# A fused attention and two expert layers on one core: decoding steps re-paced, two sums moved to VectorE, and the experts' ScalarE and VectorE put in program order

## The chip, the cores and the metric

One Trainium2 chip, one of its cores. The metric is the device time of the whole program in microseconds, from one launch. A chip core has five engines with a queue each: TensorE (PE; its weight loads are shown as PEld), VectorE (DVE), ScalarE (ACT), GpSimd (POOL) and SyncE (SP), which here only issues transfers.

## The reference, cut to what matters

Windowed attention with 32 global tokens per head feeds a dense two-matrix layer with a leaky activation, whose rows are routed to eight experts of equal capacity. Everything has fp32 inputs; `w_in`, `w_out` and `alpha` come as doubles.

```
x = attention(q_l, k_l, v_l, q_g, k_g, v_g)       # 2176 tokens x 512
h = x @ w_in                                      # 512 -> 2048
x = (max(h, 0) + alpha * min(h, 0)) @ w_out       # 2048 -> 512
logits = x @ w_gate                               # 8 experts
# pairs (token, expert) in falling order of their logit; a token takes the first
# expert that has room, and an expert has room for N / 8 = 272 tokens
for e in range(8):
    out[mask_e] = max(x[mask_e] @ w1[e], 0) @ w2[e]   # 512 -> 1024 -> 512
```

## The kernel before, in words

**Numbers.** A product of fp32 values is made from three products in the matmul's rounded type: high by high, high by low, low by high. The high half is a ScalarE copy into that type, the low half the difference of value and high half; `split` issues both, the difference on VectorE or, with `lo_eng=P`, on POOL. A weight or an activation that PE is to use is split once. The 2176 tokens are worked on in eight chunks of 272 (`CH`, also an expert's capacity, `CAP`).

**Stages.** Attention runs up to about 146 us, with the first half of the dense layer's weights decoded beside it. Then comes the dense layer's first half (hidden columns 0 to 1023): `gemm` makes, for each chunk, eight blocks of first products (12 matmuls each, L211), the activation (`neg` on ScalarE, `g` on VectorE, `ghi` on ScalarE, `glo` on POOL), and then the second products (L251): f 0 to 5 for each of four output blocks, and then f 6 and 7 for each, whose results leave as `xd` through two buffers to memory. The second half of the hidden columns follows in pairs of chunks by seven products instead of eight (`step`, L864), for which sums of quarters of the weights and of the activations are needed. Its second products (`gemm2b`, L1564; for the last chunk `last`, L1641) add to the stored part and write the rows out, turned by PE. Then each expert's slot (`slot`) makes 96 matmuls of first products (`up`, L1409) and 96 of second (`down`, L1429), eight slots in all.

**Decoding.** The doubles of the second half's weights are decoded in steps beside the dense first half: a ScalarE absolute value, then four VectorE operations on 128x512 integers, then for the quarters of `w_in` casts and differences. `parts` lists 24 such pieces; `work()` runs one step of the oldest. `turned_part` ends in two PE works of its own (L161, L168). The loop at L789 draws one point after another from `gemm`, each `yield` being one; from chunk 1 on each point adds to `due`, and if `due` is at least 1 it loses 1 and one step is issued. There are 16 points in a chunk's first products and 16 in its second, 172 steps in all.

**The first pair of chunks.** `start2` runs as the last chunk's second products begin. It lists, in `first2`, the operands and sums that the first pair of chunks of the seven products needs (`operand`: a split of 128x544 with the difference on POOL; `add2`: two sums of 128x544 on POOL), and the second products of the last chunk take one entry off at each point after f 1, 3 and 5.

**Order.** In attention PE, VectorE and ScalarE keep program order (`manual_schedule`), and from then on PE does to the end. In the dense first half and the seven products VectorE, ScalarE and POOL do too. After `order.close()` a planner orders VectorE, ScalarE and POOL by its own estimate of when an instruction can run. SP is always ordered by it. What an engine finds in its queue it runs in that order, and waits if the next is not ready.

**The router** is a generator (`router`, `phase`, `listing`) that is advanced beside the products: `advance(dt)` is called with the estimated time of what was issued, 0.113 for a matmul. An expert is closed after six rounds of two small PE works (`pc`, `pa`, L1238 and L1250) with VectorE work between them; at the end of the last round, `phase` issues a group of some twenty small VectorE operations and the next expert's best choice, then waits 2.7 for two more PE works (`pq`, L1297), and issues a second group that ends in a comparison of 128x1071 (`against`, L1204).

**Expert weights.** `fetch_1(k)` loads `w1` of an expert in four pieces of 128x1024 (512 KB each) into `raw3`, which has three buffers, and splits each (cast on ScalarE, difference on POOL); `fetch_2(k)` does so with `w2`. Both issue all four loads and splits at once: expert 0's from chunk 4 and chunk 6 of the second products on (counted from 0), expert 1's after `last`, the others as soon as the router has closed the expert and a buffer is free. `gather(k)` turns an expert's rows (L1389) through the one buffer `tx` of the pool `qx` and splits them (`xsh` on ScalarE, `xsl` on VectorE); `rows`, `tails` and `emit` (L309, L318, L1452) turn other rows through that same buffer. Four banks hold the results of `up` and `down`, in turn.

**Names of the change's steps:** `gemm1` L203, `gemm` L219, `add2` L276, `start2` L290, the pacing loop L789, `fetch_1` L1354, `fetch_2` L1368, `slot` L1488, the loop over the second products' chunks L1673, and the loop over the slots L1707.

Of the kernel before, what the change touches and what calls it, by code (L numbers as in the profile page):

```python
# [25 lines left out]
def tile_attention_moe_moe(ctx: ExitStack, tc: tile.TileContext, qkw, vw,  # L26
# [176 lines left out]
    def gemm1(c, f, g):  # L203
        _, xh, xl = X[c]
        pool, tag = odd[0] if odd and f % 2 else (pH, "h1")
        ps = pool.tile([128, CH], F32, name="h1", tag=tag)
        fs = slice(f * 128, (f + 1) * 128)
        i = 0
        for k in range(KD):
            for w, x in ((0, xh), (0, xl), (1, xh)):  # L210
                T.matmul(ps, WI[w][:, k, fs], x[:, k], start=i == 0, stop=i == 3 * KD - 1)  # L211
                i += 1
            if k % 2 == 1 and k < KD - 1:
                yield 0.7
        neg = gh_.tile([128, CH], F32, name="neg")
        A.activation(out=neg, in_=ps, func=AF.Relu, scale=-1.0)
        V.scalar_tensor_tensor(g, neg, al1[:, f:f + 1], ps, op0=OP.mult, op1=OP.add)

    def gemm(c, nxt):  # L219
# [8 lines left out]
        for f in range(KH):  # L228
            g = gh_.tile([128, CH], F32, name="g")
            yield from gemm1(c, f, g)  # L230
            split(gh[:, f], gl[:, f], g, lo_eng=P)
            yield 0.7
        if c + 1 in X:
# [9 lines left out]
        for d, fs in parts2:  # L243
            if d not in ys:
                pool, tag = (pY, "y") if d < 2 or not odd else (pH, "h1") if d == 2 else odd[0]
                ys[d] = pool.tile([128, CH], F32, name="y", tag=tag)
            ps = ys[d]
            ds_ = slice(d * 128, (d + 1) * 128)
            for f in fs:
                for i, (w, x) in enumerate(((0, gh), (0, gl), (1, gh))):  # L250
                    T.matmul(ps, WO[w][:, f, ds_], x[:, f], start=f == 0 and i == 0, stop=f == KH - 1 and i == 2)  # L251
                if f % 2 == 1 and f < KH - 1:
                    if first2 and nxt is None:
                        first2.pop(0)()
                    yield 0.7
            if fs[-1] < KH - 1:
                continue
            xd = gx.tile([128, CH], F32, name="xd", bufs=2)
            A.copy(xd, ps)  # L259
            nc.sync.dma_start(out=xpart[d, :, c * CH:(c + 1) * CH], in_=xd)  # L260
            yield 0.7
        X[c] = None
# [12 lines left out]

    def add2(i):  # L276
        a11, a12, a21, a22 = (quarter(k, t) for t in range(2) for k in range(2))
        if not i:
            P.tensor_tensor(sums[0], a21, a22, op=OP.add)
            P.tensor_tensor(sums[1], sums[0], a11, op=OP.subtract)  # L280
        else:
            P.tensor_tensor(sums[2], a11, a21, op=OP.subtract)
            P.tensor_tensor(sums[3], a12, sums[1], op=OP.subtract)

# [5 lines left out]
    def start2():  # L290
        tmp2.append(wa.tile([128, 15, CH], F32, name="tmp", tag="wa0b"))
        sums.extend(tmp2[0][:, 2 * i:2 * i + 2] for i in range(4))
        slots_.extend(gx.tile([128, 2, 2, CH], F32R, name="op", tag=t) for t in ("xh", "xl"))
        x = gx.tile([128, 2, 2, 2, CH], F32R, name="op", tag="xb1")
        slots_.extend(x[:, i] for i in range(2))
        first2.extend([lambda: operand(0, 0), lambda: operand(0, 1), lambda: add2(0), lambda: operand(0, 2),
                       lambda: operand(0, 3), lambda: add2(2)])

# [462 lines left out]
    with tc.tile_pool(name="dc2", bufs=1, side="right") as dc, tc.tile_pool(name="pW", bufs=2, space=PSUM) as pW, \  # L761
# [27 lines left out]
        while c < NCH:  # L789
            if g is None:  # L790
                g = gemm(c, c + 1 if c + 1 < NCH else None)
            while next(g, None) is not None:
                if c:
                    due += 0.82
                if due >= 1.0:
                    due -= 1.0
                    work()
            g = None
            c += 1
# [3 lines left out]
    with ExitStack() as mo:  # L803
# [542 lines left out]
        def fetch_x(k):  # L1346
# [5 lines left out]
            SLOT[k]["xg"] = xg  # L1352

        def fetch_1(k):  # L1354
            er = nc.values_load(EID[0:1, k:k + 1], engines=[mybir.EngineType.SP], min_val=0, max_val=E - 1)
# [6 lines left out]
            for kk in range(KD):  # L1362
                raw = rw.tile([128, FF], F32, name="raw3")
                nc.sync.dma_start(out=raw, in_=w1e[:, kk])
                split(t1[0][:, kk], t1[1][:, kk], raw, lo_eng=P)
            SLOT[k] = dict(w1=t1, er=er)

        def fetch_2(k):  # L1368
# [7 lines left out]
            for kk in range(0, K3, 2):  # L1376
                raw = rw.tile([128, 2, DM], F32, name="raw3")
                nc.sync.dma_start(out=raw, in_=w2e[:, kk:kk + 2])
                split(hi[:, kk:kk + 2], lo[kk // 2], raw, lo_eng=P)
            SLOT[k]["w2"] = [[hi[:, f] for f in range(K3)], [lo[f // 2][:, f % 2] for f in range(K3)]]  # L1380
# [107 lines left out]
        def slot(k):  # L1488
# [3 lines left out]
            if k == E - 1:  # L1492
                d["o"] = sl.tile([128, K3 + DM // 32, 32], F32, name="otl", tag="ot")
            f = 0
            if k == 0:
                yield from up(k, (0, 1), range(KD - 1), (0, 2))
# [3 lines left out]
            for f in range(f, K3):  # L1500
                yield from up(k, (f,), range(KD))
                if f % 2 == 0:
                    yield next(em, 0)
            d["up"] = True
            if k == E - 2:
                SLOT[k + 1]["w2f"] = wa.tile([128, K3, DM], F32, name="m2f", tag="wa1")
                w2e = w2[bass.ds(SLOT[k + 1]["er"], 1)].rearrange("e (k p) f -> p (e k) f", p=128)
                nc.sync.dma_start(out=SLOT[k + 1]["w2f"], in_=w2e)
# [78 lines left out]
        def last():  # L1587
# [71 lines left out]
            yield 0.0  # L1659

        sx = mo.enter_context(tc.tile_pool(name="sx", bufs=1))
        with tc.tile_pool(name="gb_", bufs=1) as gb_:
# [10 lines left out]
            for j, c in enumerate(ORD):  # L1673
                if j == NCH - 1:
                    while listed[0] < 1:
                        force()
                if j < NCH - 2:
                    reload(ORD[j + 2])
                for x in gemm2b(c) if j < NCH - 1 else last():
                    if j or not post:  # L1680
                        advance(x)
                    if closed[0] >= 1 and j >= 4 and 0 not in SLOT:
                        fetch_1(0)
# [3 lines left out]
        sl = mo.enter_context(tc.tile_pool(name="sl", bufs=1))  # L1687
        with tc.issue_after(SLOT[0]["cast"].ins):
            while closed[0] < 2:
                force()  # L1690
            fetch_1(1)

# [14 lines left out]
        for k in range(E):  # L1707
# [3 lines left out]
            for x in slot(k):  # L1711
                advance(x)
                n += x
                ahead(k, n)
# [4 lines left out]
                if gath is not None:  # L1719
                    left -= x  # L1720
                    if left <= 0:
                        y = next(gath, 0)
                        left = 2.2
                        n += y
                        advance(y)
            if k + 1 < E:
                while listed[0] < k + 2:
                    force()
                ahead(k, n)
                for x in gath or gather(k + 1):  # L1730
                    advance(x)


# [78 lines left out]
```

## Time and profile before

| | us |
|---|---|
| median of 3 runs (lowest, highest) | 806.62 (806.51, 807.21) |
| the profiled execution, by its own time | 805.96 |
| its span, first to last instruction | 803.9 |
| PE busy | 760.8 |
| VectorE busy | 483.5 |
| ScalarE busy | 403.5 |
| POOL busy | 413.7 |

The busy times are unions over the span. A stretch less PE's busy time in it is what PE stood idle; matmuls follow each other before the one in front has drained, so the end of each is a model, and a wait looks a little shorter than it is. The granted clock of TensorE is shown as a share of 2.4 GHz; it was 0.99 over the span. In a timeline the bracket behind a row gives how long the engine was idle before it and what ended that.

### The profile page before, as it was taken

To read this page: it belongs to the slowest core of one execution; us is meant where nothing else is said; L and a number is where in the kernel's file an instruction comes from. 1 tells how busy PE (TensorE), PEld (TensorE's weight loads), DVE (VectorE), ACT (ScalarE), POOL (GpSimd) and SP (SyncE) were. 2 spreads that over 40 slices of the span, in tenths; PEclk is the share of its full clock that TensorE was granted. 3 is DMA by queue.
4 is the path that set the end of the run, shared out by engine and by line. 5 is a ranking of instruction groups with operands and counts; after the bars stand their busy time and mean duration, and the time that the engine had idled before them with its cause. 6 is when DMAs were issued, how large, how long until landed. Compare 5 with 4: busy or idle time off the path is not lost. (4 is left out here: it accounts for less than half of the span.)

```text
span 803.9 us, 21044 instructions
## 1 busy us (share of the span) xinstructions
PE 760.8 (95%) x8258; PEld 697.8 (87%) x8258; DVE 483.5 (60%) x1672; ACT 403.5 (50%) x1018; POOL 413.7 (51%) x384
## 2 busy tenths in 40 slices
PE   6878899999999999899999999999899999999996
PEld 4656667999998999898898999998899999989994
DVE  4778897375664654266654666777567777752220
ACT  5768788345543453364565244424455554544430
POOL 2233333023311232865587348455889987788511
PEclk9999999999999999999999999999999999999999
DMA  9968894531334352125544957315467666466510
GB/s 347 404 244 326 291 345 157 164 121 55 121 113 132 119 154 84 49 71 209 195 141 124 328 182 232 93 55 163 141 188 210 211 185 194 150 188 216 174 42 28
DMA packets 55483, 139.54 MB, mean 174 GB/s; under 512 B 4952, under 2 KB 22552, under 8 KB 52569
## 3 DMA queue, kind: packets, MB, share of 16 engines
q1 hardware_dynamic: 52457, 129.30, 48.5%
q0 software_dynamic: 2928, 8.92, 3.1%
q8 instruction: 64, 1.05, 0.5%
q14 instruction: 34, 0.28, 0.1%
HBM read 113.68 MB, written 24.51 MB: 172 GB/s over the span
## 5 line engine op out<-in xcount | busy, mean ns | idle before, releaser
L74 POOL TENSOR_TENSOR m<-raw,m 128x1024 fp32r<-128x1024 f32 x64 | 152.5, 2404 | 11.3 <-ACT m L73 7.7
L74 POOL TENSOR_TENSOR glo<-g,ghi 128x272 fp32r<-128x272 f32 x64 | 55.0, 859 | 137.7 <-ACT ghi L73 137.0
L1409 PE MATMUL h<-xsh,m 128*128 128x272 f32 x512 | 105.3, 296 | 0.6 <-DVE hl L1417 0.6
L864 PE MATMUL h<-op,quad 128*128 128x272 f32 x672 | 90.3, 294 | 4.2 <-ACT g L889 2.4
L864 PEld LDWEIGHTS h<-op,quad 128*128 128x128 f32 x672 | 86.5, 191 | 8.3 <-ACT g L889 2.8
L73 ACT CAST m<-raw 128x1024 fp32r<-128x1024 f32 x64 | 65.7, 1047 | 55.6 <-DMA raw<-in_moe_w_dram 38.5
L1429 PE MATMUL h<-hh,m 128*128 128x272 f32 x448 | 92.8, 296 | 0.0
L1564 PE MATMUL h<-gr,wh 128*128 128x272 f32 x448 | 90.7, 296 | 0.0
L251 PE MATMUL y<-ghi,wout 128*128 128x272 f32 x448 | 87.0, 290 | 0.3 <-ACT ghi L73 0.3
L211 PE MATMUL h<-xh,win 128*128 128x272 f32 x448 | 86.3, 290 | 0.1
L1409 PEld LDWEIGHTS h<-xsh,m 128*128 128x128 f32 x512 | 82.5, 189 | 1.1 <-DVE hl L1417 0.9
L1409 PE MATMUL h<-xsl,m 128*128 128x272 f32 x256 | 74.1, 292 | 0.0
L1429 PEld LDWEIGHTS h<-hh,m 128*128 128x128 f32 x448 | 72.7, 190 | 0.4 <-ACT m L73 0.4
L251 PEld LDWEIGHTS y<-ghi,wout 128*128 128x128 f32 x448 | 70.9, 188 | 2.2 <-issue 1.7
L1564 PEld LDWEIGHTS h<-gr,wh 128*128 128x128 f32 x448 | 71.1, 189 | 0.9 <-ACT gr L73 0.4
L211 PEld LDWEIGHTS h<-xh,win 128*128 128x128 f32 x448 | 70.7, 188 | 0.5 <-ACT xd L259 0.3
L1429 PE MATMUL h<-hl,m 128*128 128x272 f32 x224 | 66.5, 297 | 0.0
L251 PE MATMUL y<-glo,wout 128*128 128x272 f32 x224 | 64.8, 289 | 1.5 <-POOL glo L74 1.5
L1564 PE MATMUL h<-gr,wl 128*128 128x272 f32 x224 | 65.7, 293 | 0.0
L211 PE MATMUL h<-xl,win 128*128 128x272 f32 x224 | 64.5, 288 | 0.0
L74 POOL TENSOR_TENSOR gr<-gback,gr 128x272 fp32r<-128x272 f32 x48 | 36.2, 777 | 39.7 <-ACT gr L73 39.3
L444 ACT ACTIVATE pr<-pr,mx 128x128 f32<-128x128 f32 x128 | 49.7, 394 | 13.2 <-DVE mx L442 13.1
(326 smaller groups left out, 1777.4 us busy)
## 6 DMA issues: line engine op xcount, KB each, us to landing
raw<-in_moe_w_dram SPq DMA_DIRECT2D x64, 512.0 KB, 3.7
vv<-in_v_dram SPq DMA_DIRECT2D x16, 1024.0 KB, 9.7
qk<-in_qk_dram SPq DMA_DIRECT2D x14, 720.0 KB, 7.4
raw<-in_moe_w_in_dram SPq DMA_DIRECT2D x16, 512.0 KB, 4.1
raw<-in_moe_w_out_dram SPq DMA_DIRECT2D x16, 512.0 KB, 3.6
xs<-xb SPq DMA_DIRECT2D x16, 272.0 KB, 6.7
xpart<-xd SPq DMA_DIRECT2D x32, 136.0 KB, 2.8
xb<-xs SPq DMA_DIRECT2D x4, 1088.0 KB
```

Of the source, the lines that this page charges most:

```text
L73: a = A.copy(hi, src)
L74: return a, (lo_eng or V).tensor_tensor(lo, src, hi.bitcast(F32), op=OP.subtract)
L211: T.matmul(ps, WI[w][:, k, fs], x[:, k], start=i == 0, stop=i == 3 * KD - 1)
L251: T.matmul(ps, WO[w][:, f, ds_], x[:, f], start=f == 0 and i == 0, stop=f == KH - 1 and i == 2)
L444: A.activation(out=sc, in_=sc, func=AF.Exp, bias=d["mx", j][:, ii:ii + 1], scale=-1.0, accum_out=d["sm", j][:, ii:ii + 1])
L864: T.matmul(ps, w[a][kk][:, q * 128:(q + 1) * 128], x[:, b, kk], start=fresh and m == 0, stop=m == 5, skip_group_check=not fresh)
L1409: T.matmul(ps, d["w1"][w][:, kk, f * 128:(f + 1) * 128], x[:, kk], start=kk == 0 and i == 0, stop=kk == KD - 1 and i == 2)
L1429: T.matmul(ps, d["w2"][w][f][:, ms], x[:, f], start=i == 0, stop=i == 3 * K3 - 1)
L1564: T.matmul(ps[j], (woh, wol)[w][f][:, ds_], x, start=f == 0 and a == 0, stop=f == KH - 1 and a == 2)
```

## The change

The points of `gemm` now yield 0.5 in the first products and 1.3 in the second, and the loop adds what is yielded to `due`. `add2` takes an engine; the first pair's sums go to VectorE, at the first and fourth of now four entries of `first2`. `fetch_1` and `fetch_2` only list their pieces: `load_more` keeps up to three of them in flight, and `pace(x)`, called with the same estimated times as `advance`, splits the oldest when 2.5 have passed since the last split and 4.5 since its load was issued; `flush` splits what is left of one set before it is used. From the last chunk of the second products on, VectorE and ScalarE keep program order (`order2`). The last slot's small block `otl` moves into the tile of `m2f`, and the fetch of expert 1 is no longer queued behind the last cast.

```diff
 gemm1 / gemm (first products)
-                yield 0.7
+                yield 0.5
 gemm (second products, both places)
-                    yield 0.7
+                    yield 1.3

-    def add2(i):
+    def add2(i, eng=None):
+        eng = eng or P
...
-            P.tensor_tensor(sums[0], a21, a22, op=OP.add)
-            P.tensor_tensor(sums[1], sums[0], a11, op=OP.subtract)
+            eng.tensor_tensor(sums[0], a21, a22, op=OP.add)
+            eng.tensor_tensor(sums[1], sums[0], a11, op=OP.subtract)
...
-        first2.extend([lambda: operand(0, 0), lambda: operand(0, 1), lambda: add2(0), lambda: operand(0, 2),
-                       lambda: operand(0, 3), lambda: add2(2)])
+        first2.extend([lambda: (add2(0, V), operand(0, 0)), lambda: operand(0, 1), lambda: operand(0, 2),
+                       lambda: (add2(2, V), operand(0, 3))])

-            while next(g, None) is not None:
+            for x in g:
                 if c:
-                    due += 0.82
+                    due += x

+        pieces, loaded, clock = [], [], [0.0, 0.0]
+
+        def load_more():
+            while pieces and len(loaded) < 3:
+                p = pieces.pop(0)
+                raw = rw.tile([128, 1024], F32, name="raw3")
+                p["raw"] = raw if p["n"] == 1 else raw.rearrange("p (k d) -> p k d", k=p["n"])
+                nc.sync.dma_start(out=p["raw"], in_=p["src"])
+                p["at"] = clock[0]
+                loaded.append(p)
+
+        def split_one():
+            p = loaded.pop(0)
+            split(p["hi"], p["lo"], p["raw"], lo_eng=P)
+            clock[1] = clock[0]
+            load_more()
+
+        def pace(dt=0.0):
+            clock[0] += dt
+            if loaded and clock[0] >= clock[1] + 2.5 and clock[0] >= loaded[0]["at"] + 4.5:
+                split_one()
+
+        def flush(key):
+            while any(p["key"] == key for p in loaded + pieces):
+                split_one()

 fetch_1 (fetch_2 in the same way, in pairs of blocks)
             for kk in range(KD):
-                raw = rw.tile([128, FF], F32, name="raw3")
-                nc.sync.dma_start(out=raw, in_=w1e[:, kk])
-                split(t1[0][:, kk], t1[1][:, kk], raw, lo_eng=P)
+                pieces.append(dict(key=(k, 1), n=1, src=w1e[:, kk], hi=t1[0][:, kk], lo=t1[1][:, kk]))
+            load_more()

 slot
+            flush((k, 1))      # before up
+            flush((k, 2))      # after up
-                d["o"] = sl.tile([128, K3 + DM // 32, 32], F32, name="otl", tag="ot")
+                d["o"] = d["otl"]
...
+        def order2():
+            mo.enter_context(tc.manual_schedule(engines={mybir.EngineType.DVE, mybir.EngineType.Activation}))
 loop over the second products' chunks
                 if j == NCH - 1:
                     while listed[0] < 1:
                         force()
+                    flush((0, 1))
...
+                if j == NCH - 1:
+                    order2()
                 for x in gemm2b(c) if j < NCH - 1 else last():
                     if j or not post:
                         advance(x)
+                    pace(x)

-        with tc.issue_after(SLOT[0]["cast"].ins):
-            while closed[0] < 2:
-                force()
-            fetch_1(1)
+        while closed[0] < 2:
+            force()
+        fetch_1(1)
 loop over the slots: pace(x) or pace(y) behind each advance
```

## Rows read from the trace of the kernel before

**Rows 1.** Windows by stage: busy us (x instructions) per engine, clock, DMA

```profile
146.50:332.20 185.70, 183.20 (x1431) 178.67 (x1430) 105.35 (x186) 82.53 (x192) 53.95 (x61) 1.00 0.37 117
...
332.20:438.30 106.10, 101.68 (x859) 93.21 (x858) 62.22 (x167) 58.96 (x156) 74.61 (x71) 0.98 0.40 135
...
438.30:540.10 101.80, 101.33 (x943) 97.39 (x941) 67.22 (x290) 35.83 (x80) 54.66 (x62) 1.00 0.55 181
...
540.10:563.40 23.30, 21.29 (x180) 20.00 (x180) 16.54 (x63) 9.46 (x19) 13.18 (x11) 1.00 0.57 171
...
563.40:778.00 214.60, 209.70 (x1816) 203.39 (x1815) 121.51 (x490) 103.64 (x184) 168.07 (x93) 0.99 0.57 175
```

**Rows 2.** Groups, dense half: busy us, mean ns | idle before, causes

```profile
L216 ACT ACTIVATE neg<-h 128x272 f32<-128x272 f32 x56 | 21.8, 390 | 0.4 <-PE h L211 0.3
...
L217 DVE SCALAR_TENSOR_TENSOR g<-neg,al,h 128x272 f32<-128x272 f32 x56 | 27.7, 494 | 38.9 <-ACT neg L216 30.2 <-POOL glo L74 8.3
...
L73 ACT CAST ghi<-g 128x272 fp32r<-128x272 f32 x56 | 23.5, 420 | 44.1 <-DVE g L217 44.1
...
L259 ACT COPY xd<-y 128x272 f32<-128x272 f32 x24 | 9.0, 385 | 28.0 <-PE y L251 13.8 <-DMA xpart<-xd 11.5 <-PE h L211 2.6
```

**Rows 3.** Timeline, chunks 3 and 4 of the dense half: PE, VectorE

```profile
218.51 0.39 PE L251 MATMUL y<-glo,wout 128*128 128x272 f32 x1 [0.57 <-POOL glo L74]
...
243.99 1.20 DVE L94 SCALAR_TENSOR_TENSOR wts<-raw,wts 128x512 int32<-128x512 int32 x1
...
247.09 1.29 DVE L74 TENSOR_TENSOR xl<-xb,xh 128x1088 fp32r<-128x1088 f32 x1 [1.49 <-ACT xh L73]
...
249.94 0.69 DVE L94 SCALAR_TENSOR_TENSOR wts<-raw,wts 128x512 int32<-128x512 int32 x1
...
250.69 1.04 PE L161 MATMUL wp<-wts,ag 128*32 128x512 f32 x2 [0.45 <-DVE wts L94]
```

**Rows 4.** Timeline where the seven products begin: ScalarE, PE

```profile
331.30 1.19 ACT L73 CAST op<-tmp 128x544 fp32r<-128x544 f32 x2 [6.02 <-POOL tmp L280]
...
333.11 1.77 PE L864 MATMUL h<-op,quad 128*128 128x272 f32 x12 [0.87 <-ACT xd L259]
...
334.62 0.86 ACT L259 COPY xd<-y 128x272 f32<-128x272 f32 x2 [1.56 <-DMA xpart<-xd]
...
336.99 1.27 PE L864 MATMUL h<-op,quad 128*128 128x272 f32 x4 [2.11 <-ACT g L889]
```

**Rows 5.** Timeline of the last chunk's first turns: POOL, PE, ScalarE

```profile
536.62 7.11 POOL L74 TENSOR_TENSOR m<-raw,m 128x1024 fp32r<-128x1024 f32 x3
...
542.48 0.65 PE L309 MATMUL yt<-ident,pt 128*128 128x128 f32 x4 [0.28 <-ACT yr L311]
...
543.13 1.05 ACT L73 CAST m<-raw 128x1024 fp32r<-128x1024 f32 x1 [0.71 <-DMA raw<-in_moe_w_dram]
...
544.72 0.65 PE L318 MATMUL yt<-ident,xtail 128*112 128x128 f32 x4 [0.83 <-ACT yr L311]
```

**Rows 6.** Timeline in slots 0 and 4: ScalarE, PE

```profile
576.10 1.04 ACT L73 CAST m<-raw 128x1024 fp32r<-128x1024 f32 x1 [4.37 <-DMA raw<-in_moe_w_dram]
...
578.03 0.18 PE L1250 MATMUL pa<-sat,ones 128*128 128x8 bf16 x1 [1.99 <-DVE sat L1243]
...
708.97 0.63 PE L1389 MATMUL xt<-ident,xg 128*128 128x128 f32 x4 [1.06 <-issue]
```

**Rows 7.** Timeline at the slots' first and third closings: VectorE, PE

```profile
583.70 0.17 DVE L1253 TENSOR_SCALAR_CACHE_REDUCE home<-pa 128x8 f32<-128x8 f32 x1 [0.94 <-PE pa L1250]
...
589.39 0.29 DVE L1215 TENSOR_TENSOR ohs<-oh,home 128x136 bf16<-128x136 f32 x1
...
590.49 0.60 PE L1389 MATMUL xt<-ident,xg 128*128 128x128 f32 x4
...
591.33 1.28 DVE L1204 TENSOR_TENSOR gs<-home,thr 128x1071 bf16<-128x1071 f32 x1
...
658.23 0.60 PE L1452 MATMUL ox<-ident,ot 128*128 128x128 f32 x4
```

More of the change, by code (lines that the diff above doesn't have):

```diff
@@ L231, in gemm @@
             split(gh[:, f], gl[:, f], g, lo_eng=P)
-            yield 0.7
+            yield 0.5
         if c + 1 in X:
@@ L254, in gemm @@
                         first2.pop(0)()
-                    yield 0.7
+                    yield 1.3
             if fs[-1] < KH - 1:
@@ L260, in gemm @@
             nc.sync.dma_start(out=xpart[d, :, c * CH:(c + 1) * CH], in_=xd)
-            yield 0.7
+            yield 1.3
         X[c] = None
@@ L274, in load2 @@
         nc.sync.dma_start(out=raw2(), in_=xs[:, :, 2 * p * CH:(2 * p + 2) * CH].rearrange("k p t -> p k t"))
-    def add2(i):
+    def add2(i, eng=None):
+        eng = eng or P
         a11, a12, a21, a22 = (quarter(k, t) for t in range(2) for k in range(2))
         if not i:
-            P.tensor_tensor(sums[0], a21, a22, op=OP.add)
-            P.tensor_tensor(sums[1], sums[0], a11, op=OP.subtract)
-        else:
-            P.tensor_tensor(sums[2], a11, a21, op=OP.subtract)
-            P.tensor_tensor(sums[3], a12, sums[1], op=OP.subtract)
+            eng.tensor_tensor(sums[0], a21, a22, op=OP.add)
+            eng.tensor_tensor(sums[1], sums[0], a11, op=OP.subtract)
+        else:
+            eng.tensor_tensor(sums[2], a11, a21, op=OP.subtract)
+            eng.tensor_tensor(sums[3], a12, sums[1], op=OP.subtract)
     def operand(p, j):
@@ L1376, in fetch_2 @@
             for kk in range(0, K3, 2):
-                raw = rw.tile([128, 2, DM], F32, name="raw3")
-                nc.sync.dma_start(out=raw, in_=w2e[:, kk:kk + 2])
-                split(hi[:, kk:kk + 2], lo[kk // 2], raw, lo_eng=P)
+                pieces.append(dict(key=(k, 2), n=2, src=w2e[:, kk:kk + 2], hi=hi[:, kk:kk + 2], lo=lo[kk // 2]))
+            load_more()
             SLOT[k]["w2"] = [[hi[:, f] for f in range(K3)], [lo[f // 2][:, f % 2] for f in range(K3)]]
@@ L1504, in slot @@
             d["up"] = True
+            flush((k, 2))
             if k == E - 2:
-                SLOT[k + 1]["w2f"] = wa.tile([128, K3, DM], F32, name="m2f", tag="wa1")
+                t = wa.tile([128, K3 * DM + 32 * K3 + DM], F32, name="m2f", tag="wa1")
+                SLOT[k + 1]["w2f"] = t[:, :K3 * DM].rearrange("p (k d) -> p k d", d=DM)
+                SLOT[k + 1]["otl"] = t[:, K3 * DM:].rearrange("p (a b) -> p a b", b=32)
                 w2e = w2[bass.ds(SLOT[k + 1]["er"], 1)].rearrange("e (k p) f -> p (e k) f", p=128)
@@ L1712, in tile_attention_moe_moe @@
                 advance(x)
+                pace(x)
                 n += x
@@ L1725, in tile_attention_moe_moe @@
                         advance(y)
+                        pace(y)
             if k + 1 < E:
@@ L1731, in tile_attention_moe_moe @@
                     advance(x)
+                    pace(x)
 _INS = ['qk', 'v', 'moe_w_in', 'moe_w_out', 'moe_w_out_t', 'gate', 'moe2_w1', 'moe2_w2']
```

## The prediction, made before the changed kernel was seen running

> **What bounds the kernel now.** I read the busy times by stage first [rows 1]. TensorE is the bound in every stage but the first, which the change does not touch. From 146.5 us on, a stretch less its PE busy time is what could be won at all: 2.5 us in the dense first half (146.5 to 332.2), 4.4 in the seven products, 0.5 in the second products up to 540.1, 2.0 in the last chunk and 4.9 in the experts up to 778. A wait costs a little more than its idle time: in the dense half 1431 matmuls fill 183.2 us, 0.128 us from start to start, but each is drawn at 0.29 or 0.39, so I add about 0.25 us to a wait there. Then I read, in the timeline of PE, what ended each wait, and followed it back on the engine that was late. No stage has a second bound: the reader is to see a few long waits, each with a queue behind it that stood in the wrong order.
>
> **Part 1, the decoding's pace (dense half, chunks 1 to 7).** A chunk has 16 pace points in its first products and 16 in its second. Before, each adds 0.82: 13.1 steps in either phase. After, 0.5 and 1.3. But at most one step runs at a point, so the second phase runs 16 and carries 4.8 over, and the next first phase runs 12 or 13 steps again, one at each of its first nine or ten points and one at every second after that. So the title's move happens fully only in chunk 1; elsewhere 3 steps are added to the second phase, the first phase's load moves to its front, and the 172 steps end in chunk 7's first phase (5 of them) instead of its second (2 of them).
>
> What a step costs there: per block f, ScalarE and VectorE hand over neg, g and ghi (0.39, 0.49, 0.42 us), then POOL makes glo [rows 2]; with the hand-overs the loop is 1.35 us against 1.51 for PE's 12 matmuls. VectorE is free for some 0.85 us of it: one of its steps hides there (0.69 to 1.20 for the longest, [rows 3]), two do not, and a step on ScalarE always lengthens the loop. PE wants glo of f=5 2.0 us into the second phase, so a lateness of some 2.5 us is free. Before, chunk 3 passed that (0.57 us idle for glo [rows 3]) as did, by 0.4 to 0.5, chunks 4 and 7. With the after order, the loop sums to f=5 are 3.0, 1.8, 1.3, 1.6 and 0.2 us of growth for chunks 2 to 6, on 0.4 to 1.2 us that the chunk begins late because ScalarE's third xd waits for a transfer (the xd row of [rows 2]). That gives new waits of 0.9 (chunk 2), 0.3 (3), 0.2 (5), none in 4, 6 and 7. Gone: 1.8 us of idle in five waits, 2.6 with the correction. The turned product wp waited 0.45 for the last VectorE step [rows 3]; its four steps' lead shrinks from 4.9 points to 4, and the chunk's xl (1.29) stands in front of it, so I charge 0.65 more. Together -2.6 + 1.4 + 0.65 = **-0.6 us** (bounds -2.5, if the front-loading lets the queue catch up, to +1.5, if wp waits for a whole backlog).
>
> One rule bears on this. The last decode step took 1.20 us at 243.99, beside a glo, and 0.69 at 249.94, alone (two of eight such rows) [rows 3]. The Trainium skill (SBUF — State Buffer, Terms) has VectorE and GpSimd take one port pair by a lock for a whole instruction, the loser blocked fully; that would make it some 1.34, near the 1.20 measured. By it, VectorE's new sums beside POOL's operands could each be held for one POOL instruction of 1.35 us; they would still be ready 4 us before PE asks for them, and the sum stays.
>
> **Part 2, the first pair's sums on VectorE.** Before, POOL ran both sums between its operand differences, and ScalarE stood 6.02 us at a cast that needed them; the xd copies behind it came late, the third then waited 1.56 us for its transfer, and PE idled 0.87 and 2.11 us [rows 4]. With the corrections that is 3.3 to 3.6 us. After, VectorE has no decoding left here, so the two sums run at once. No row shows such an add on VectorE; the nearest, xl of twice the length at 1.29 [rows 3], gives 0.65, POOL's own 1.35 is the upper bound; either is done some 3.5 to 5 us into the phase. ScalarE's casts then end before the phase does, POOL's four differences (1.35 each) finish 3 us earlier than the sums let them before, and the first two xd leave as soon as PE ends them. What is late next: the last two xd still wait for the first two transfers (1.8 us here), and the fourth operand's cast (0.65) stands before the copy that PE wants: 0.6 us is left of the 2.11. **-2.7 us** (bounds -1.0 and -3.3).
>
> **Part 3, the last chunk, now in program order.** The second weights' pieces of expert 0 enter at the start of the chunk before. By the pace (first after 4.5, then every 2.5, in steps of 0.113 and 0.4) the first three fall at 4.6, 7.2 and 9.8 of that chunk's 12.05, the fourth at 12.4: three matmuls into the last chunk, where ScalarE keeps program order. Its raw buffer comes free only when POOL has done the first piece (536.62 + 2.4, held up by the spilled chunk's buffer, which no edit touches), so it lands at 543.1 as before [rows 5]. Before, ScalarE made a row copy meanwhile and waited 0.71. After, it stands at the cast from 540.5 to 544.1, the first row copy ends at 544.7, and the second turn, which shares that copy's only buffer, waits 2.55 us on PE instead of 0.28, the tail turn 0.3 instead of 0.83 [rows 5]. **+1.75 us**, and +0.2 where VectorE now finishes a listing step (1.2 us) before the first sum of the gathered rows. Bounds: 0, if the piece slips in ahead of the boundary, and +3.
>
> **Part 4, the experts.** What goes: ScalarE stood 4.37 us at a cast whose piece had not landed, relu and hl behind it, and PE idled 1.99 for a router sum; a like wait brought PE's 1.06 at a gather [rows 6]. Paced pieces wait 4.5 after issue and 2.5 between; a matmul counts 0.113 there and takes 0.128, so that is 2.8 us against POOL's 2.4 a piece, and ScalarE meets few that have not landed. The two waits go, 3.55 us with the correction; of the other 1.85 us of idle time, some ten small waits worth up to 2.9, I take 1.85. **-5.4 us** (bounds -2 to -6.5).
>
> What comes: when the router closes an expert it traces two groups of VectorE work in one go: some 4.6 us after the last sum and 3.1 us after the ranks. Before, the planner slipped a gather's difference, a copy or an hl between them [rows 7]: the first group runs from 583.70 to 589.39 + 0.29, less a slipped-in xsl and two short waits, the second from there to the end of the 1.28 us comparison at 591.33. In program order the slipped-in work stands behind. At the first closing both groups end at 583.7 + 7.7 = 591.4 and the gather's xsl (half of xl, 0.65) at 592.0; PE's next turn, due at 590.49, waits for it: 1.55 us. At the second closing (same pattern, one group) I get 1.3. At the third the first group starts 3.3 us before the row turn due at 658.23; 4.6 us of it and the last output block's copy of 0.5 go ahead of that turn: 1.8 us. Two closings fall where four product banks (4.5 us of PE) cover the late hl: nothing. **+4.65 us** (bounds 0 and +12).
>
> Parts 1 to 4: -0.6 - 2.7 + 1.95 - 0.75 = -2.1 us on the profiled execution's own 805.96, so 803.9. The median of the runs shown, 806.62, is 0.66 above that execution; I add it: **804.5 us**. About 0.2%, 1.6 us, is what a measurement of this kernel can tell from no change.
>
> **Rivals.** *A, program order is nearly free (0.28).* If the difference behind a closing is not on PE's path and the fourth piece finds its place, the +4.65 and +1.95 fall away and the last chunk's own 0.8 goes too: 804.5 - 7.4 = 797.1. For it: VectorE is busy 121.5 of 214.6 us in the experts [rows 1], and a gather's turns come 3 us apart (20 matmuls of 0.128 and the turn), which covers a single group's rest. Against it: the two groups together fill 7.7 us without a gap.
>
> *B, slower: VectorE in program order at the closings (0.17).* If each of the five closings makes PE wait for what 7.7 us of router work exceed two turn spacings less the turns' own work (5.3) by, 2.4 us, that is 12 us instead of 4.65: 811.9. It decides from 8.4 us of such waits on (4.65 + 2.1 + 1.6). For it: hl and the copies are traced all through the closings. Against it: the banks cover 4.5 us.
>
> *C, the pace does not do what it says (0.15).* The carry of 4.8 brings the first phases their old load at a worse place: the waits of part 1 become +1.5 instead of -0.6, and the experts' new waits eat the old: 804.5 + 2.1 = 806.6, no change.
>
> **How the numbers follow.** My forecast has 0.40, its own range 802 to 807. Faster by over 0.2% (under 805.0): all of A, 0.6 of mine, little of C: 0.54. Within: 0.35 of mine, most of C: 0.25. Slower: B and the rests: 0.21. The range 797.5 to 809.5 leaves out half of A's lower side and B's upper.
>
> **What would show it.** Part 1: the waits for glo in chunks 3, 4 and 7 gone, one in chunk 2, and a longer wait at the second phase's wp in chunk 4. Part 2: VectorE rows of 0.65 us at the sums, ScalarE without the 6 us, PE idle under 1 us at 334. Part 3: a ScalarE wait of over 2 us for a piece at the last chunk's start, PE idle 2 us or more at a row turn. Part 4: no ScalarE wait of 3 us or more for a piece; PE waits of 1 us or more at a gather turn behind a closing. I am wrong if PE's idle time in the experts falls under 2 us (A) or passes 9 (B).

## The result and the profile after: slower by 1.2%

After: 817.39 us median of 6 runs (814.51 to 820.82). Before, on the same chip: 807.99 (6 runs, 806.51 to 810.43). The ratio is 1.0117, 95% interval 1.0086 to 1.0148. The forecast was 804.5 in a range of 797.5 to 809.5.

The profiled execution after has a span of 816.3 us, 12.4 more than before's. I cut both traces at the start of each stage's first matmul; chunks are counted from 0. The attention part, which no edit touches, differs by up to 3.6 us between the executions profiled here, so I compare lengths of stages, not times of day.

| stage | before, us | after, us | difference | forecast |
|---|---|---|---|---|
| chunks 1 to 6 | 151.96 | 161.97 | +10.0 | about -0.2 |
| chunk 7 and the seven products | 128.66 | 123.35 | -5.3 | -3.1 |
| second products | 104.96 | 105.02 | +0.1 | 0 |
| last chunk | 23.13 | 30.05 | +6.9 | +1.95 |
| slots and end | 240.44 | 241.30 | +0.9 | -0.75 |

(The forecast's part 1 is split here: its waits of chunk 7, 0.4 us, stand in the second row.)

Windows of the trace after, as [rows 1], for chunks 2, 3, 4, 5 and 7, the products, the last chunk, slots 0 to 6:

```profile
178.78:207.40 28.62, 25.65 (x195) 24.42 (x194) 18.28 (x32) 13.52 (x31) 6.71 (x8) 1.00 0.30 92
207.40:231.73 24.33, 24.33 (x195) 24.20 (x193) 15.74 (x28) 12.35 (x28) 6.81 (x8) 1.00 0.38 111
231.73:263.06 31.33, 28.72 (x207) 26.32 (x206) 16.99 (x31) 12.06 (x29) 6.74 (x8) 0.95 0.36 109
263.06:290.15 27.09, 25.47 (x195) 24.39 (x193) 16.65 (x31) 11.58 (x27) 6.72 (x8) 1.00 0.35 109
316.58:340.75 24.17, 24.17 (x194) 24.17 (x193) 11.94 (x17) 10.12 (x25) 12.93 (x12) 1.00 0.15 48
340.75:439.93 99.18, 97.39 (x831) 90.15 (x829) 60.08 (x162) 56.12 (x147) 66.57 (x63) 1.00 0.40 135
544.95:575.00 30.05, 23.85 (x180) 22.64 (x180) 16.71 (x61) 9.07 (x19) 13.23 (x11) 0.89 0.45 130
575.00:782.08 207.08, 199.84 (x1749) 193.68 (x1747) 123.19 (x485) 101.05 (x174) 166.01 (x91) 1.00 0.59 180
```

Read the first two numbers of a row against each other: PE was idle 3.0 us in chunk 2, 2.6 in chunk 4, 1.6 in chunk 5 and 6.2 in the last chunk (before: 0, 1.0, 0 and 1.9). Then the clock: 0.95 in chunk 4 and 0.89 in the last chunk, 1.00 in both before. There PE also worked slowly.

**Chunk 2.** ScalarE's timeline at its start (178.78), to set beside the xd row of [rows 2]; then SP's:

```profile
177.19 0.37 ACT L259 COPY xd<-y 128x272 f32<-128x272 f32 x1
179.72 0.62 ACT L124 CAST quad<-mag 128x512 fp32r<-128x512 f32 x1 [2.16 <-DVE mag L94]
180.24 0.67 ACT L259 COPY xd<-y 128x272 f32<-128x272 f32 x2
...
184.40 0.39 ACT L259 COPY xd<-y 128x272 f32<-128x272 f32 x1 [2.91 <-DMA xpart<-xd]
184.68 0.40 ACT L216 ACTIVATE neg<-h 128x272 f32<-128x272 f32 x1
```

```profile
179.71 0.33 SPq L80 DMA_DIRECT2D raw<-in_moe_w_in_dram  x1
180.65 4.48 SPq L260 DMA_DIRECT2D xpart<-xd  x3
```

and the view of transfers for 176 to 190 us (count, KB each, median us from issue to landing):

```profile
xpart<-xd SPq DMA_DIRECT2D x4, 136.0 KB, 3.6
```

The first xd copy is out at 177.19. The second and third stand behind a cast that waits 2.16 us for VectorE; meanwhile SP has issued the next raw load of the decoding (512 KB), and the two xd transfers are queued behind it. With two buffers the fourth copy waits for one of them, and the chunk's first neg stands behind that copy. The first block's products end 1.51 us into a chunk; I call what neg starts later than that its lateness. Here it is 184.68 - 178.78 - 1.51 = 4.4 us. For chunks 2 to 7:

| first neg late, us | 2 | 3 | 4 | 5 | 6 | 7 |
|---|---|---|---|---|---|---|
| before | 0.9 | 1.8 | 1.1 | 0.2 | 0.2 | 3.7 |
| after | 4.4 | 1.0 | 2.4 | 4.2 | 1.8 | 1.1 |

In three of these twelve a raw load is issued between a chunk's first and second xd transfer: the 4.4, the 4.2 (the second transfer takes 5.52 us there) and before's 3.7, of which SP's rows are

```profile
305.04 0.33 SPq L260 DMA_DIRECT2D xpart<-xd  x1
305.46 1.42 SPq L80 DMA_DIRECT2D raw<-in_moe_w_out_dram  x1
306.97 4.78 SPq L260 DMA_DIRECT2D xpart<-xd  x3
```

**Long waits of PE after,** in its timeline: the turned product wp [rows 3], the last chunk [rows 5] and three closings [rows 7]:

```profile
252.48 1.33 PE L161 MATMUL wp<-wts,ag 128*32 128x512 f32 x2 [2.29 <-DVE wts L94]
...
549.00 0.66 PE L310 MATMUL yt<-ident,pt 128*128 128x128 f32 x4 [2.16 <-ACT yr L312]
...
564.45 0.52 PE L1624 MATMUL yt<-ident,pt 128*128 128x128 f32 x3 [1.96 <-DVE pt L1683]
...
571.05 0.90 PE L1624 MATMUL yt<-ident,pt 128*128 128x128 f32 x3 [2.08 <-DVE pt L1683]
...
599.91 0.66 PE L1414 MATMUL xt<-ident,xg 128*128 128x128 f32 x4 [1.58 <-DVE xsl L74]
...
633.79 0.42 PE L1414 MATMUL xt<-ident,xg 16*128 16x16 f32 x4 [1.36 <-DVE xsl L74]
...
670.67 0.33 PE L1477 MATMUL ox<-ident,ot 128*128 128x128 f32 x1 [1.20 <-DVE ot L1458]
```

The wait at 549.00 and the last three had been forecast (2.55, 1.55, 1.3, 1.8). The two for pt had not. VectorE's timeline shows what is ahead of pt (columns as above):

```profile
559.11 0.16 DVE L1244 SCALAR_TENSOR_TENSOR sat<-pc,lack 63x8 bf16<-63x8 f32 x1
560.93 0.17 DVE L1254 TENSOR_SCALAR_CACHE_REDUCE home<-pa 128x8 f32<-128x8 f32 x1 [1.66 <-PE pa L1251]
...
561.90 1.27 DVE L1205 TENSOR_TENSOR gs<-home,th 128x1071 bf16<-128x1071 f32 x1
...
563.86 0.43 DVE L1683 TENSOR_TENSOR pt<-h,pt 128x272 f32<-128x272 f32 x1
```

A router round was written ahead of the sum pt. In program order VectorE stood 1.66 us for the router's own PE work, pa, then did the round, and only then the sum whose result PE's next turn was waiting for.

**What a wait costs.** PE's clock around the wait that ends at 571.05 (windows: us, PE busy, clock, DMA):

```profile
568.00:570.00 2.00, 0.98 (x8) 1.00 0.00 0
570.00:571.00 1.00, 0.00 (x0) 0.78 0.00 0
571.00:574.00 3.00, 2.94 (x13) 0.51 0.00 0
574.00:575.00 1.00, 1.00 (x10) 1.00 0.43 123
```

PE was idle from 568.97 to 571.05; the clock fell from 2.4 to 1.2 GHz at 570.56, stayed there for some 3.4 us, and rose again once PE had worked. Of the 3.4 us, 2.9 lie behind the wait; half of that, some 1.5 us, is lost on top of the wait of 2.08. The same happened behind the waits that end at 252.48 and at 549.00, and not behind the one at 564.45.

### The profile page after: what moved, and what is told of

Read it like the earlier page. It is cut to its first block, busy times and chain, and to the rows that moved or that the text cites. A ratio compares the mean times of both kernels' runs of the same rounds, so it can differ in the third digit from the quotient of the medians.

```text
span 816.3 us, 21071 instructions
## 1 busy us (share of the span) xinstructions
PE 764.2 (94%) x8258; PEld 699.8 (86%) x8258; DVE 492.1 (60%) x1676; ACT 403.7 (49%) x1018; POOL 406.8 (50%) x380
## 5 line engine op out<-in xcount | busy, mean ns | idle before, releaser
L74 POOL TENSOR_TENSOR glo<-g,ghi 128x272 fp32r<-128x272 f32 x64 | 52.6, 822 | 146.6 <-ACT ghi L73 146.0
```

What stands on the lines that cost most here:

```text
L74: return a, (lo_eng or V).tensor_tensor(lo, src, hi.bitcast(F32), op=OP.subtract)
```

## The experiments

The first four columns of numbers come from the traces (difference of a stage's length from before's, us), the last two from the timed runs. The second products stay within 0.6 us everywhere. Each ratio is to runs of the kernel before on the same chip, whose median is 805.8 to 808.0 us. A trace is one execution, and not always one near the median: chunks 1 to 6 come out at +10.0 in after and at +7.1 in order_late, which has no other edit there, so a share of the 10.0 is good to some 3 us.

| run | chunks 1-6 | 7, products | last chunk | slots, end | median us | ratio to before (95%) |
|---|---|---|---|---|---|---|
| after | +10.0 | -5.3 | +6.9 | +0.9 | 817.39 | 1.0117 (1.0086, 1.0148) |
| p_back | +1.4 | -3.5 | +5.9 | -0.1 | 811.50 | 1.0042 (1.0019, 1.0066) |
| p_alone | +7.8 | -5.2 | +0.3 | +2.3 | 810.46 | 1.0027 (1.0001, 1.0053) |
| xd4 | +1.2 | -6.1 | +5.6 | +0.4 | 809.38 | 1.0029 (1.0007, 1.0051) |
| order_late | +7.1 | -5.0 | +0.8 | +0.1 | 810.37 | 1.0041 (1.0020, 1.0063) |
| no_carry | +0.8 | -0.6 | +5.4 | -0.1 | 813.29 | 1.0065 (1.0026, 1.0104) |
| before_xd4 | -2.3 | -1.0 | +0.2 | -0.5 | 802.85 | 0.9939 (0.9912, 0.9966) |
| xd4_late | +0.6 | -5.7 | -0.2 | +1.7 | 803.53 | 0.9967 (0.9943, 0.9991) |
| xd4_act | +0.7 | -6.0 | +2.0 | -1.8 | 802.23 | 0.9931 (0.9904, 0.9958) |
| raw_hold | +7.5 | -5.7 | +4.7 | +0.2 | 815.92 | 1.0117 (1.0077, 1.0156) |
| raw_after | +3.0 | -5.4 | +4.6 | +0.1 | 810.30 | 1.0069 (1.0044, 1.0095) |
| best_act | -2.3 | -5.9 | +0.3 | -4.6 | 794.75 | 0.9835 (0.9799, 0.9872) |
| best_plan | -2.3 | -6.0 | +2.5 | -1.1 | 802.67 | 0.9939 (0.9914, 0.9964) |

**p_back: the old pace in the changed kernel.**

```diff
-                    due += x
+                    due += 0.82
```

> The changed kernel with the old pace (0.82 at every point), all else as changed. By the milestones of the two traces, chunks 1 to 6 of the dense half are 9.9 us longer after the change, chunk 7 and the start of the products 2.3 shorter, the products 3.0 shorter. Theory 1 (the pace alone costs the 9.9; the sums on VectorE earn the 5.3): 817.4 - 9.9 = 807.5, the last chunk's 6.9 and the experts stay. Theory 2 (5.3 of the gain come from a chunk 7 free of decoding, which the old pace takes away): 817.4 - 9.9 + 2.5 = 810. If the pace were not the cause: 817.

Chunks 1 to 6 fall from +10.0 to +1.4: the pace is the cause there. Of the 5.3 us gained in chunk 7 and the products 3.5 stay, between the two theories. The median, 811.50, is above the second one's 810 as well.

**p_alone: the new pace in the kernel before**, with the yields of 0.5 and 1.3 and nothing else of the change.

```diff
-                    due += 0.82
+                    due += x
```

> The kernel before with the new pace alone. Theory 1 (the pace costs 9.9 us by itself): 808.0 + 9.9 = 818, less at most 2.3 at the start of the products if VectorE and ScalarE free of decoding there also help the old order of the sums: 815.6 to 818. If the dense half was lengthened by something else in the change: 808.

Chunks 1 to 6 are +7.8, as theory 1 has it in kind. The time misses it: 810.46, not 815.6 to 818. For chunk 7 and the products are 5.2 shorter, not 2.3 at most, although POOL still makes the sums, and the traced execution, 812.11 us, is itself 1.65 above the median. POOL starts the first pair's differences 15.2 us into chunk 7 instead of 18.7; whether that comes from the missing decoding or from a first neg that is 1.0 us late instead of 3.7 was not taken apart. ScalarE still stands at the cast of a sum,

```profile
335.70 1.20 ACT L73 CAST op<-tmp 128x544 fp32r<-128x544 f32 x2 [5.17 <-POOL tmp L280]
```

and PE idles only 0.55 us behind it: ScalarE's long wait was not by itself the price. So pace and sums buy the same waits; the sums alone (p_back) are worth 3.5, both together 5.3. Products windows of p_alone, then of p_back:

```profile
339.24:438.58 99.34, 97.39 (x830) 90.15 (x829) 60.18 (x162) 56.04 (x147) 69.07 (x65) 1.00 0.39 134
```

```profile
336.77:436.27 99.50, 97.46 (x831) 90.22 (x829) 61.02 (x164) 56.23 (x147) 67.06 (x64) 1.00 0.40 134
```

Both are as short as after's 99.18 (before: 102.23, at a clock of 0.98). The slots of p_alone hold no edit and are 2.3 longer: PE waits of 2.38 and 1.82 us there are each followed by half the clock, where before had one such wait (1.99). Why they are longer stays open.

**xd4: four buffers for xd.**

```diff
-            xd = gx.tile([128, CH], F32, name="xd", bufs=2)
+            if d < 2:
+                xd = gx.tile([128, CH], F32, name="xd", bufs=2)
+            else:
+                xd = gh_.tile([128, CH], F32, name="xd", tag="neg" if d == 2 else "g")
```

> The changed kernel with four buffers instead of two for xd (the last two copies of a chunk go to the idle buffers of neg and g), so that no xd copy waits for the transfer of an earlier one. Theory H (ScalarE reaches the next chunk's first neg late because the third and fourth xd stand behind transfers of 2 to 3.7 us that were themselves delayed by casts): the 2.9 us wait in front of chunk 2 goes, and with it 3 to 6 us of the 9.9: 811 to 814. Rival C (the carry of 4.8 steps at the front of the first phases): no change, 817.

More than expected: 8.8 of the 10.0 us go. ScalarE at the start of its chunk 2 (179.34), and the windows of chunks 2 and 4:

```profile
180.36 0.38 ACT L262 COPY xd<-y 128x272 f32<-128x272 f32 x1
181.11 0.40 ACT L216 ACTIVATE neg<-h 128x272 f32<-128x272 f32 x1 [0.37 <-PE h L211]
```

```profile
179.34:204.32 24.98, 24.54 (x195) 24.28 (x194) 17.45 (x30) 13.35 (x31) 6.72 (x8) 1.00 0.34 103
...
228.48:256.24 27.76, 26.83 (x206) 24.93 (x205) 16.39 (x30) 11.96 (x29) 6.85 (x8) 1.00 0.40 123
```

The cast still stands ahead of the copies, but nothing waits for a transfer: neg now waits for PE, 0.3 us behind the products, in every chunk. What idle time is left in the dense half is 0.44 for glo in chunk 2, 0.45 in chunk 5 and 0.93 for wp: within half a microsecond of what part 1 had forecast (0.9, 0.2 and 1.1). The carry of 4.8 steps is still in this kernel.

**order_late: program order from the first slot on.**

```diff
-                if j == NCH - 1:
-                    order2()
...
         g2.close()
         sl = mo.enter_context(tc.tile_pool(name="sl", bufs=1))
+        order2()
```

> The changed kernel with program order on ScalarE and VectorE from the first expert on instead of from the last chunk on. Theory V (program order on VectorE holds the last chunk's sums pt behind the router's groups, two PE waits of 2.0 us; and ScalarE's row copy behind the fourth piece's cast, 2.2 us): 5 of the last chunk's 6.9 us go, 812.4. Rival (the pieces issued two chunks early take the time, by raw buffers and POOL): the last chunk stays some 5 us longer than before, 816.

The last chunk is +0.8, with PE waits of 0.28 and 0.64 at the row turns and none over 0.2 for pt:

```profile
545.51 0.65 PE L310 MATMUL yt<-ident,pt 128*128 128x128 f32 x4 [0.28 <-ACT yr L312]
...
547.55 0.65 PE L319 MATMUL yt<-ident,xtail 128*112 128x128 f32 x4 [0.64 <-ACT yr L312]
```

Theory V; the early pieces themselves cost little. The median, 810.37, is under the 812.4 of theory V, helped by chunks 1 to 6, which are 2.9 shorter than after's by no edit of this run.

**no_carry: what is due is cut to 0.99 after each step** (first-phase yields 0.56).

```diff
-                    due -= 1.0
+                    due = min(due - 1.0, 0.99)
```

> The changed kernel with the carry cut off (what is due is capped at 0.99 after each step, 0.56 instead of 0.5 in the first phases so that all 172 steps still fit): 9 steps in a first phase instead of 12 or 13, and none of them packed at its front; the second phases still run a step at each of their 16 points. Theory H (the third and fourth xd, behind transfers and casts, make the next chunk's first neg late): chunk 2 still begins late and is 3 to 4.4 us longer than before, chunks 1 to 6 together 6 to 10 us longer; 814 to 817. Rival C (the steps packed at the front of the first phases do it): chunks 1 to 6 within 2 us of before, 809.

Each theory gets half. ScalarE at the start of its chunk 2 (182.25):

```profile
188.26 0.39 ACT L259 COPY xd<-y 128x272 f32<-128x272 f32 x1 [3.07 <-DMA xpart<-xd]
188.54 0.40 ACT L216 ACTIVATE neg<-h 128x272 f32<-128x272 f32 x1
```

The lateness arises without any carry (188.54 - 182.25 - 1.51 = 4.8 us), and chunks 1 and 2 together are 3.6 longer. But chunks 3 to 6 come out 2.8 shorter than before, so the sum is +0.8, not the 6 to 10 that I expected of H: there are fewer steps at the front of the first products, and wp comes only in chunk 5 and does not wait. As far as this run and xd4 show, the loss takes both, the late start and the packed steps. The saving returns in the products (-0.6 instead of -5.3): decoding steps are left over, VectorE still runs them at 340, and PE waits 3.19 us behind it for a copy of the products' own (L908).

**raw_hold and raw_after: the raw load out of the way.** raw_hold holds the call that starts the next decoding back while a chunk's xd copies are issued; raw_after also ties it in SP's queue behind the last xd transfer, `sent[0]`:

```diff
-                    ahead2()
+                    with tc.issue_after(sent[0].ins):
+                        ahead2()
```

> The changed kernel with two xd buffers as it has, where the decoding's next raw load (512 KB) is not issued between a chunk's first and last xd transfer but right after the last; steps, pace and order stay. Theory Q (the third and fourth xd wait because a raw load stands in the transfers' way, which makes the xd transfer of 1.7 to 2.4 us one of 3.7 to 5.5): the first neg of chunks 2 and 5, now 4.4 and 4.2 us late, comes 1 to 2.4 us late as in the other chunks, and of the 9.9 us of chunks 1 to 6 some 5 go: 812. Theory W (ScalarE's casts in front of the xd copies, which wait for VectorE, are enough): the two negs stay over 3.5 us late, 816 to 817.

> As raw_hold, but each held raw load is tied in the queue behind the last xd transfer's issue, so that the four xd transfers of a chunk stand in a row (in the run raw_hold the raw load was still issued between the first and the last: 0.73 us behind chunk 2's start and 1.20 in front of chunk 5's). Theory Q: the first negs of chunks 2 and 5, 4.4 and 4.2 us late after the change, come 1 to 2.4 us late, and 4 to 6 of the 9.9 us of chunks 1 to 6 go: 811 to 813. Theory W (the casts in front of the xd copies are enough): both stay over 3.5 us late, 816 to 817.

raw_hold moved nothing: SP's order is the planner's, and the load was still issued 0.73 us into chunk 2. It says nothing on Q. In raw_after (chunk 2 starts at 179.61) SP has

```profile
177.98 4.49 SPq L262 DMA_DIRECT2D xpart<-xd  x4
182.56 2.73 SPq L80 DMA_DIRECT2D raw<-in_moe_w_in_dram  x2
```

and ScalarE

```profile
178.98 0.62 ACT L124 CAST quad<-mag 128x512 fp32r<-128x512 f32 x1 [1.03 <-DVE mag L94]
...
181.74 0.39 ACT L261 COPY xd<-y 128x272 f32<-128x272 f32 x1 [0.98 <-DMA xpart<-xd]
182.02 0.40 ACT L217 ACTIVATE neg<-h 128x272 f32<-128x272 f32 x1
```

The xd transfers take 1.7 to 1.8 us there instead of 3.65, the negs of chunks 2 and 5 are 0.9 and 0.3 late instead of 4.4 and 4.2, and 7.0 of the 10.0 us go. Theory Q; what stays is mostly wp's 2.28 us and the clock behind it. The Trainium skill (DMA: Bandwidth & Descriptors, Two DMAs through the same engine are not ordered) has descriptors within one queue of one DMA engine start in order; by it a small store behind a large load waits its turn. These rows agree: 1.7 to 1.8 us ahead of the load, 3.65 behind it.

**before_xd4: the four buffers alone, in the kernel before** (the diff of xd4).

> The kernel before with four xd buffers and nothing else. If the waits of xd for its transfers cost something under the old pace too (0.87 us of PE idle at the products' start, up to 0.4 per chunk): 3 us less, 804. If the old pace hides them (PE's idle in chunks 3, 4 and 7 is for glo, and the 2.11 us at the products for an operand's cast): 806.7, no change.

Slightly better than the first theory: 0.6% faster. But the 0.87 and 2.11 at the products stay (0.91 and 2.09): the gain is the glo waits of chunks 3, 4 and 7 [rows 3], which were the end of the same xd waits. I had read them as the loop's load.

**xd4_late and xd4_act: the two causes together.** xd4_late has the edits of xd4 and order_late; xd4_act keeps `order2` at the last chunk, for ScalarE alone:

```diff
-            mo.enter_context(tc.manual_schedule(engines={mybir.EngineType.DVE, mybir.EngineType.Activation}))
+            mo.enter_context(tc.manual_schedule(engines={mybir.EngineType.Activation}))
```

> Four xd buffers and program order from the first expert on, both at once. If the two causes are apart (the dense half and the last chunk share nothing), the savings add: by the traces 816.3 - 9.2 in the dense half - 6.1 in the last chunk = 801 of span, 803 to 804 by the time shown, 3 us under the kernel before. If one hides the other: 809.

> Four xd buffers, and program order from the last chunk on for ScalarE alone; VectorE stays with the planner. Theory V (VectorE's program order makes the two waits of 2.0 us in the last chunk and the three of 1.58, 1.36 and 1.20 us in the experts): those five, 8.2 us, go, and the wait of 2.16 us behind the fourth piece's cast stays; 801 to 803. Rival (it is ScalarE's program order that costs): the last chunk stays 5 us longer than before, 808.

Both as the first theory: span 800.6 against 801 forecast, and in xd4_act the five VectorE waits are gone while the one of ScalarE stays (2.27); one of 1.82 for a router's sum, followed by half the clock, comes in slot 2.

**best_act and best_plan: the old pace, four buffers, sums on VectorE, paced pieces.** best_act joins the diffs of p_back, xd4, order_late and xd4_act; best_plan has no `order2` at all.

> The old pace, four xd buffers, sums on VectorE, paced pieces, and program order from the first expert on for ScalarE alone. If the savings seen one by one add: 2.6 us from the four buffers under the old pace, 3.5 at the products from the sums on VectorE, 1.9 in the experts: span 803.9 - 8 = 796, 798 to 799 by the time shown. If the sums and the four buffers buy the same waits at the products: 801 to 802.

> As the run with program order for ScalarE alone, but no program order at all behind the products: the planner keeps both engines, and of the experts' edits only the paced pieces stay. If the pacing is what takes ScalarE's waits for pieces away (before: one of 4.37 us and PE idle 1.99 behind it): the same 798 to 799. If program order on ScalarE is needed for that: 1 to 3 us more, 800 to 802.

best_act is 1.65% faster than before, more than the sum: the slots give 4.6 instead of 1.9. An estimated 1.7 of the 4.6 (half of 3.4) is the half clock behind before's wait of 1.99, which is gone with the wait. Its windows of chunk 7, the products, the last chunk and slots 0 to 6:

```profile
306.15:330.32 24.17, 24.17 (x195) 24.17 (x193) 16.91 (x24) 11.47 (x27) 14.43 (x12) 1.00 0.23 70
330.32:428.87 98.55, 97.15 (x830) 90.09 (x829) 60.88 (x164) 55.75 (x146) 66.81 (x64) 1.00 0.40 135
...
534.27:557.72 23.45, 21.59 (x180) 19.99 (x181) 16.34 (x62) 9.46 (x19) 13.02 (x11) 1.00 0.57 168
557.72:759.04 201.32, 198.85 (x1749) 193.48 (x1747) 119.65 (x485) 101.39 (x173) 166.34 (x91) 1.00 0.60 185
```

No PE wait in the slots is longer than 0.7 us. Without program order on ScalarE (best_plan) waits of 1.92 and 1.45 us stand at the end of the last chunk and in the first slot: the second theory.

## Why the prediction was wrong

**Part 1 is the step that failed,** +10.0 us in chunks 1 to 6 against -0.2: "on 0.4 to 1.2 us that the chunk begins late because ScalarE's third xd waits for a transfer". The lateness was 4.4, 1.0, 2.4, 4.2 and 1.8 us for chunks 2 to 6, and in chunks 2 and 5 it is the fourth xd that waits. I took the xd row of [rows 2], a wait of 11.5 us over 24 copies, as a constant of the chunk's end. It is one of three things in a row: a decoding step at each of the last four points, so that copies stand behind a cast; a raw load that a finished piece starts there, ahead of the copies' transfers; and two buffers. Before's own chunk 7 (3.7 us late) had shown it. The loop sums built on that start held to within half a microsecond, as xd4's remaining waits show; the wait for wp was right in kind, but it was 2.3 us, not 1.1. One count was off, without effect: the waits for ghi and glo that were to go are four (0.27, 0.57, 0.52 and 0.43), not five, and 0.25 on each makes 2.8, not 2.6.

**The size of a wait** was wrong twice. I added 0.25 us to each. A wait can also bring half the clock behind it, which added 0.7 to 1.5 us to the stages below. The wp wait of 2.28 made chunk 4 29.8 us long at a clock of 1.00 (p_alone, raw_hold) and 31.3 at 0.95 (after, order_late, raw_after). The last chunk's three waits made it 27.8 long at 1.00 (raw_hold, raw_after), 28.5 to 29.0 at 0.94 (xd4, p_back, no_carry), 30.05 at 0.89.

**Part 2** was right in what it does: no 6 us on ScalarE, PE idle 0.54 at the products' start. That the 6 us were the price it had wrong: in p_alone ScalarE stands 5.17 there, and PE idles 0.55. The four sums took 0.72, 1.22, 1.88 and 1.88 us, not 0.65, without harm. The gain over the old pace is 3.5, above the bound of 3.3 since the half clock behind before's 2.11 us wait went too; but the pace alone buys the same waits, which I had not seen; so the total of this stage came out better than forecast by luck in part.

**Part 3 failed too.** It had PE's wait behind ScalarE right (2.16 against 2.55) and left out VectorE: I counted one listing step of 1.2 us ahead of one sum and not the router's rounds that stand ahead of two, 1.96 and 2.08. PE's idle time rose from 1.9 to 6.2 us, and the half clock added 2.6 to its busy time: +6.9 against +1.95.

**Part 4:** the new waits are 1.58, 1.36 and 1.20 us, 4.1 together against 4.65. What went is 4.1 less the 0.9 that the stage is longer, 3.2 instead of 5.4 and within the bounds: the waits of [rows 6] are gone, and small ones of 0.2 to 0.8 are new. Some 1.5 of the 3.2 is clock, which the forecast did not have: in slots 0 to 6 PE was busy for 201.32 us before, with half the clock behind the wait of 1.99, and for 199.84 after. Rival B had the right engine and order but put the price into the slots; half of it fell in the last chunk (1.96 and 2.08, against 4.1 in the slots). Its 811.9 came nearer to the measured time, but most of the loss is in chunks 1 to 6, where it had none. Rival C named the stage, at +1.5 us; its carry is real but needs the late start.

## What to carry to other kernels

When steps are spread over a loop, look at its last points first: what ScalarE must still hand over there, in how many buffers, and what else is started on the same transfer queue between them. Two more buffers there gave back as much as the old pace did (8.8 against 8.6 us), and won 2.3 us under the old pace too. Program order for an engine is as good as the order in which the program is written: it helped on ScalarE in the slots, where waits for loads had been planned badly, cost 2.3 us on ScalarE in the last chunk, and cost on VectorE, where a round that itself waits for PE stood ahead of sums that PE wanted. Price a long wait on PE with the clock rows behind it: here half the clock cost up to 1.5 us on top of a wait of 2.3, in some executions and not in others.

## What the hardware showed that I had not expected

- The same wait (2.28 us at wp) was followed by half the clock in three executions and not in two; 1.96 us at 564.45 was not, 2.08 at 571.05 was. Nor does the length decide: in xd4_late half the clock came behind a wait of 1.36 us that ends at 616.73 (windows: us, PE busy, clock, DMA), and behind the same wait in no other execution:

```profile
615.00:617.00 2.00, 0.64 (x7) 1.00 0.54 98
...
618.00:621.00 3.00, 3.00 (x15) 0.50 0.74 257
```

What does decide is not shown here.
- VectorE's sums beside POOL's differences take 1.88 us, and 0.72 alone; the rows are after's:

```profile
330.52 0.72 DVE L280 TENSOR_TENSOR tmp<-xb 128x544 f32<-128x544 f32 x1
331.27 1.22 DVE L281 TENSOR_TENSOR tmp<-tmp,xb 128x544 f32<-128x544 f32 x1
332.41 1.88 DVE L283 TENSOR_TENSOR tmp<-xb 128x544 f32<-128x544 f32 x1
```

POOL's two differences beside them took 3.64 together, 1.82 each, 1.35 before. So 1.35 was no upper bound for VectorE, and POOL was slower beside it as well. The Trainium skill (SBUF — State Buffer, Terms) has the loser blocked for the other's whole instruction: 0.65 and 1.35 give an estimate of 2.0, and the 1.88 measured is nearer to it than to the bound that I took from rows.
- An xd transfer of 136 KB takes 1.7 us with a free queue, 3.65 (chunk 2) and 5.52 (chunk 5) behind a load of 512 KB.
